# K and V stores moved from SyncE's queue to GpSimd's, loads issued at the first free slot, weight gradients stored whole

## The chip, the cores and the metric

The kernel runs on one core of one Trainium2 chip. The core has five instruction queues that matter here: TensorE (PE), VectorE (DVE), ScalarE (ACT), GpSimd (POOL) and SyncE (SP). Transfers between memory (HBM) and on-chip memory (SBUF) are issued from a queue and carried by 16 DMA engines that serve the whole core. The metric is the device time of one launch in microseconds (us). Before the change it is 729.72 us, the median of three runs (728.75 to 731.86).

## The reference

The reference is the forward pass and the gradient of a decode block with one token (x has 640 numbers). A layer norm of x feeds two branches that are added to x: attention of one query per head over a cache (32 heads, 8192 keys, 128 numbers each), and a gated MLP (640 to 1728 and back). In short:

```
q = xn @ wq                       # 32 heads x 128
p_h = softmax(q_h . K_h / sqrt(128));  o_h = p_h @ V_h
out = x + concat(o) @ wo + (silu(xn@w1) * (xn@w3)) @ w2
# gradients of everything, from grad_out:
dV_h = outer(p_h, do_h)           # 8192 x 128 per head
dK_h = outer(u_h, q_h)            # u_h = p_h * (V_h.do_h - p_h.(V_h.do_h))
dwq, dwo, dw1, dw3, dw2 and dx    # dw* are outer products too
```

All tensors are bf16. K and V are 2 MB (2,097,152 bytes) per head each, and the gradients dK and dV are just as large. So 64 tiles of 2 MB are read and 64 are written; the profile counts 151.34 MB read and 151.34 MB written in all.

## The kernel before

**Slots.** SBUF holds ten slots of 2 MB (`free_slots`, L116). A slot is a tile of 128 partitions by 8192 numbers (16,384 bytes per partition). K or V of a head is loaded into a slot, used there, and then overwritten in place by its own gradient (`outer`, L464: two DVE instructions of 128x4096 per tile, L466), which is stored from the same slot (`store`, L477). The slot then goes to the end of `free_slots` and takes a later head's K or V (`load_next`, L122). Four of the slots first hold the MLP's weights (mA to mD); the MLP is done between heads 1 and 2 (`mlp`, L557), its weight gradients are stored from GpSimd, and the slots then join the others.

**A head.** `head(h)` (L746) writes the order of the work by hand. PE transposes pieces of K (`T`, L314, PE L318 with the ACT copy L320), multiplies them with the query (`Mp`, L339), then the same for V; DVE does the softmax; PE sums with the tile as the moving operand (`wsum`, L433). The outer products of head h-1 run during head h: `outers_a` (L734) at its start makes dV, stores it, and makes half of dK; `outers_b` (L740) in its middle makes the rest of dK and stores it. The first transposes of the next head's K lie at the end of a head. So K of a head is held from shortly before its head to the middle of the next, and V from the middle of its head to the start of the next.

**Weight groups.** wq and wo are loaded by groups of four heads (`load_group`, L109: 640 KB each, three buffers per tensor in `wpool`). Group g+1 is first read in the third head of group g (`prep_do`, DVE L257, called from `side_v`) and multiplied in its fourth (`prep_q`). When a group is done, wo is overwritten by its gradient (`fin_wo`, L518) in the first head of the next group, and wq in pieces (`fin_wq`, L524) in the second and third. The last of the five pieces is made in the middle of the third head; then wq's gradient is stored and group g+3 is loaded into the freed buffers, from GpSimd.

**Queues.** A transfer is issued when its queue reaches it and everything it waits for has come. Within a queue nothing overtakes. Before the change SP issues all loads and all stores of K and V (`fifo`, L104), in the order store, load, store, load; a load waits there until the store that empties its slot has landed. `load_next` issues a load only when at least three slots are free (`lag[0] = 3`, L160), so a load goes into the slot whose store was issued two stores earlier. GpSimd's queue issues the loads and stores of the weight groups and of the MLP's gradients. The weight gradients are split (`store_group`, L505): for groups 1 to 5, wq's 128 rows go as 5 rows and 121 rows from GpSimd and 2 rows from SP; in the last group both tensors go as 68 rows from SP and 5 and 55 rows from GpSimd.

Transfers from SP are described by hardware (the profile's queue q1, hardware_dynamic), those from GpSimd by software on GpSimd (q0, software_dynamic). Each of the 16 DMA engines keeps one list of packets for each of the two. Completion is counted on eight marks in turn for each of the two kinds, so a transfer also waits for the landing of the eighth one before it of its kind.

Of the kernel before, what the change touches and what calls it, by code (L numbers as in the profile page):

```python
# [16 lines left out]
P = 128  # L17
# [4 lines left out]
def kernel(  # L22
# [22 lines left out]
    nc = tc.nc  # L45
# [8 lines left out]
    GH = 4  # L54
    NG = H // GH
    GW = GH * DH
# [19 lines left out]
    dkc = out_2.rearrange("b h (p j) d -> (b h) p (j d)", p=P)  # L76
    dvc = out_3.rearrange("b h (p j) d -> (b h) p (j d)", p=P)
    wq_v = A_wq.rearrange("(ci p) n -> p ci n", p=P)
    wo_v = A_wo.rearrange("(h p) c -> p h c", p=P)
    dwq_v = out_4.rearrange("(ci p) n -> p ci n", p=P)  # L80
    dwo_v = out_5.rearrange("(h p) c -> p h c", p=P)
# [22 lines left out]
    def fifo(out_, in_):  # L104
        nc.sync.dma_start(out_, in_)
# [3 lines left out]
    def load_group(g, eng):  # L109
        wq_g = wpool.tile([P, NC, GW], BF16, name="wq_g", tag="wq_g")  # L110
        eng.dma_start(wq_g[:], wq_v[:, :, g * GW:(g + 1) * GW])
        wo_g = wpool.tile([P, GH, D], BF16, name="wo_g", tag="wo_g")
        eng.dma_start(wo_g[:], wo_v[:, g * GH:(g + 1) * GH, :])
        grp[g] = dict(wq=wq_g, wo=wo_g)

    free_slots = [kvpool.tile([P, KVN], BF16, name=f"kv{i}", tag=f"kv{i}") for i in range(NSLOT)]  # L116
    kv_tiles = {}
    pending = [("K", h) if k == 0 else ("V", h) for h in range(H) for k in range(2)]

    lag = [1]  # L120

    def load_next():  # L122
        if not pending or len(free_slots) < lag[0]:
            return
        kind, h = pending.pop(0)
        t = free_slots.pop(0)
        fifo(t[:], (kc if kind == "K" else vc)[h])
        kv_tiles[(kind, h)] = t

    load_next()  # L130
    load_group(0, nc.sync)
    for _ in range(3):
        load_next()
# [22 lines left out]
    fifo(w3b, w3_v[:, NA, :])  # L156
    for _ in range(2):
        load_next()

    lag[0] = 3  # L160

    ident_f = consts.tile([P, P], F32, name="ident_f")
    make_identity(nc, ident_f[:])
# [83 lines left out]
    def prep_new(g):  # L247
        G_ = grp[g]
        G_["cb"] = wpool.tile([P, 2, GH], BF16, name="cb", tag="cb")
        G_["do"] = wpool.tile([P, GH], F32, name="do_c", tag="do_c")  # L250
        G_["cm"] = wpool.tile([P, 2, 2, GH, 2], BF16, name="cm_g", tag="cm_g")
        G_["od"] = wpool.tile([P, GH, 2], F32, name="od_g", tag="od_g")

    def prep_do(g, hh):
        G_ = grp[g]
        junk = small.tile([P, D], BF16, name="side", bufs=1)
        nc.vector.scalar_tensor_tensor(junk[:], G_["wo"][:, hh, :], 1.0, g_bc[:], ALU.mult, ALU.mult,  # L257
                                       accum_out=G_["do"][:, hh:hh + 1])
        if hh == GH - 1:
            nc.vector.tensor_copy(G_["cb"][:, 1, :], G_["do"][:])  # L260
# [24 lines left out]
    def prep_cm(g, ps):  # L285
        nc.vector.tensor_tensor(grp[g]["cm"][:].rearrange("p t a h m -> p (t a h) m"),
                                ps.unsqueeze(2).to_broadcast([P, 4 * GH, 2]),
                                mask2.unsqueeze(1).to_broadcast([P, 4 * GH, 2]), ALU.mult)
# [188 lines left out]
    def store(kind, h):  # L477
        t = kv_tiles.pop((kind, h))
        if kind == "K":
            hd.pop(h)  # L480
        fifo((dkc if kind == "K" else dvc)[h], t[:])
        free_slots.append(t)
        load_next()

# [17 lines left out]
        for hh in range(GH):  # L502
            out_row(G_["od_bf"][:, hh, 0:1], G_["wo"][:, hh, :])

    def store_group(g, dst, t, split=False):  # L505
        if split:
            for lo, hi in ((0, 5), (5, 126)):
                nc.gpsimd.dma_start(dst[lo:hi], t[lo:hi])
            fifo(dst[126:P], t[126:P])
            return  # L510
        if g < NG - 1:
            nc.gpsimd.dma_start(dst, t[:])
            return
        fifo(dst[0:68], t[0:68])
        for lo, hi in ((68, 73), (73, P)):
            nc.gpsimd.dma_start(dst[lo:hi], t[lo:hi])

    def fin_wo(g):  # L518
        G_ = grp[g]
        for hh in range(GH):  # L520
            nc.vector.tensor_scalar(G_["wo"][:, hh, :], g_bc[:], G_["od"][:, hh, 0:1], None, ALU.mult)
        store_group(g, dwo_v[:, g * GH:(g + 1) * GH, :], G_["wo"])

    def fin_wq(g, ci):  # L524
        G_ = grp[g]
        wq_g, dqb = G_["wq"], G_["dqb"]
        nc.vector.scalar_tensor_tensor(wq_g[:, ci, :], wq_g[:, ci, :], 1.0, dqb, ALU.mult, ALU.mult,  # L527
                                       accum_out=dxa[:, ci, g:g + 1])
        nc.vector.tensor_scalar(wq_g[:, ci, :], dqb, xn_col[:, ci:ci + 1], None, ALU.mult)
        if ci == NC - 1:  # L530
            store_group(g, dwq_v[:, :, g * GW:(g + 1) * GW], wq_g, 1 <= g <= 5)
            grp.pop(g)
            if g + 3 < NG:
                load_group(g + 3, nc.gpsimd)

    def wrow(wi, ci):
        if ci < NA:
# [146 lines left out]
    def side_k(h):  # L684
        g, hh = divmod(h, GH)
        if hh == 1 and g > 0:
            fin_wq(g - 1, 0)
        elif hh == 2 and g > 0:
            fin_wq(g - 1, 3)
        elif hh == 3 and g + 1 < NG:  # L690
            prep_do(g + 1, 1)

    def side_m(h):
        g, hh = divmod(h, GH)
        if hh == 0 and g > 0:
            fin_od(g - 1)
        elif hh == 1 and g > 0:
            fin_wq(g - 1, 1)
        elif hh == 2 and g > 0:
            fin_wq(g - 1, 4)  # L700
        elif hh == 3 and g + 1 < NG:
            prep_do(g + 1, 2)
            prep_do(g + 1, 3)

    def side_v(h):
        g, hh = divmod(h, GH)
        if hh == 0 and g > 0:
            fin_wo(g - 1)
        elif hh == 1 and g > 0:
            fin_wq(g - 1, 2)  # L710
        elif hh == 2 and g + 1 < NG:
            prep_new(g + 1)
            prep_do(g + 1, 0)
        elif hh == 3 and g + 1 < NG:
            prep_cm(g + 1, hd[h]["m"][:, 324:324 + 4 * GH])

    def side_pe1(h):
        g, hh = divmod(h, GH)
        if hh == 0 and g > 0:
            fin_pe(g - 1)  # L720
        elif hh == 3 and g + 1 < NG:
            prep_q(g + 1)
# [11 lines left out]
    def outers_a(h):  # L734
        outer_v(h, 0, J // 2)
        outer_v(h, J // 2, J)
        store("V", h)
        outer_k(h, 0, J // 2)

    def outers_b(h):  # L740
        outer_k(h, J // 2, J)
        store("K", h)
# [3 lines left out]
    def head(h):  # L746
# [39 lines left out]
        Mp(h, "V", 4)  # L786
        side_pe2(h)
        side_v(h)
        if nxt:
            fill_qz(h + 1)  # L790
# [45 lines left out]
    fin_od(NG - 1)  # L836
    fin_pe(NG - 1)
    fin_wo(NG - 1)
    for ci in range(NC):
        fin_wq(NG - 1, ci)  # L840
# [58 lines left out]
```

## Time and profile before

| | before |
|---|---|
| median of three runs | 729.72 us |
| the profiled execution's own time | 730.06 us |
| its span in the profile | 728.3 us |
| PE, DVE, ACT, POOL busy | 82%, 63%, 52%, 5% |
| bytes moved, mean rate | 303.53 MB, 417 GB/s |
| mean granted TensorE clock | 0.927 |

The page cuts the span into 40 slices; a digit is the busy share of an engine in tenths, and the DMA line is the mean of the 16 DMA engines. Queue lines give packets, megabytes and the time that the packets took as a share of 16 engines' span. A line of waits gives the waiting engine and line, what it waited for, the total in us, the number of waits and the longest. A line of a table of windows gives, for a stretch of the span, the busy time of PE, PE's weight loads, DVE, ACT and POOL with their instruction counts, then the granted clock, the DMA share and GB/s. Lines of DMA issues end with the median time from issue to landing.

### The profile page before, as it was taken

What the parts mean: (1) busy time and instruction counts of PE and PEld (TensorE: products, weight loads), DVE (VectorE), ACT (ScalarE), POOL (GpSimd) and SP (SyncE); (2) the same over time, 40 slices, a digit from 0 to 9 for tenths busy, and PEclk for the clock granted to TensorE, in tenths of its full rate; (3) what the DMA queues carried; (4) which work ended last, traced back from release to release, by engine and by line L of the source; (5) the groups of instructions that cost most, each with busy time, mean ns of one, the idle gap of its engine ahead of it and who ended that gap; (6) DMA issues with size and microseconds to landing.
All of it is one profiled execution on the core that took longest, in us unless ns stands there. A gap on an engine that the chain in (4) does not pass through costs nothing.

```text
span 728.3 us, 12951 instructions
## 1 busy us (share of the span) xinstructions
PE 600.8 (82%) x5193; PEld 375.6 (52%) x5193; DVE 460.1 (63%) x811; ACT 375.7 (52%) x727; POOL 35.0 (5%) x52
## 2 busy tenths in 40 slices
PE   3989589999999999877986889878896987988840
PEld 2547456665566556544554555445563555644520
DVE  4169646677767886767556746556755665677482
ACT  3640736665666656544554546455562555645410
POOL 0010110000100000000010000000000000000000
PEclk9996799999999999999999989999998999999975
DMA  9999999999999999999999999999999999999996
GB/s 347 398 409 424 427 428 428 413 427 425 418 409 429 427 426 424 423 429 422 425 425 427 431 420 427 421 427 432 410 428 424 428 425 422 429 424 430 429 415 239
DMA packets 28358, 303.53 MB, mean 417 GB/s; under 512 B 3481, under 2 KB 5532, under 8 KB 11658
## 3 DMA queue, kind: packets, MB, share of 16 engines
q1 hardware_dynamic: 22022, 277.14, 90.4%
q0 software_dynamic: 6272, 25.56, 8.8%
q8 instruction: 41, 0.67, 0.4%
q14 instruction: 19, 0.16, 0.1%
q10 hardware_dynamic: 4, 0.00, 0.0%
HBM read 151.34 MB, written 151.34 MB: 416 GB/s over the span
## 4 chain that ended last, share of the span: by engine, by line
DMA 57%; PE 33%; DVE 5%; ACT 2%; issue 1%; SPq 0%; ACTq 0%; DVEq 0%
DMA out_dram<-kv 30%; DMA kv<-in_A_k_cache_dram 18%; PE pT L318 15%; DMA kv<-in_A_v_cache_dram 7%; PE sA L339 4%; PE X L433 3%; PE dA L339 3%; DVE kv L466 2%; PE m L356 2%; DMA wo_g<-in_A_wo_dram 2%; ACT KT L320 1%; PE gu_ps L562 1%; PE dh_ps L573 1%; DVE side L257 0%; PE pT L266 0%
## 5 line engine op out<-in xcount | busy, mean ns | idle before, releaser
L320 ACT COPY KT<-pT 128x512 f32<-128x512 f32 x512 | 287.7, 587 | 230.9 <-PE pT L318 210.3
L318 PE MATMUL pT<-ident_f,kv 128*128 128x128 f32 x2048 | 306.6, 289 | 61.6 <-DMA kv<-in_A_k_cache_dram 29.9
L318 PEld LDWEIGHTS pT<-ident_f,kv 128*128 128x128 f32 x2048 | 236.2, 148 | 155.1 <-issue 59.6
L466 DVE TENSOR_TENSOR kv<-qd,U 128x4096 bf16<-128x4096 bf16 x64 | 146.0, 2283 | 0.0
L466 DVE TENSOR_TENSOR kv<-qd,P 128x4096 bf16<-128x4096 bf16 x64 | 143.5, 2283 | 0.0
L433 PE MATMUL X<-kv,Z 128*32 128x512 bf16 x1024 | 93.5, 402 | 1.8 <-DVE Z L450 1.8
L339 PE MATMUL sA<-KT,qz 128*32 128x512 bf16 x512 | 83.9, 408 | 0.0
L339 PE MATMUL dA<-KT,qz 128*32 128x512 bf16 x512 | 83.3, 404 | 0.0
L416 DVE SCALAR_TENSOR_TENSOR U<-m,P 128x64 bf16<-128x64 f32 x32 | 7.5, 234 | 83.0 <-PE m L356 83.0
L382 DVE TENSOR_REDUCE mrow<-m 128x1 f32<-128x64 f32 x32 | 7.2, 223 | 75.1 <-PE m L356 75.0
L339 PEld LDWEIGHTS <-qz 128*32 128x32 bf16 x1024 | 29.6, 95 | 40.4 <-issue 37.7
L433 PEld LDWEIGHTS <-Z 128*32 128x32 bf16 x1024 | 32.4, 99 | 33.8 <-issue 5.7
L356 PE MATMUL m<-selc,KT 64*128 64x64 f32 x256 | 30.7, 243 | 8.6 <-ACT KT L346 8.6
L356 PEld LDWEIGHTS m<-selc,KT 64*128 64x128 f32 x256 | 21.7, 145 | 30.4 <-ACT KT L346 21.6
L376 ACT CAST qd<-pT 128x256 bf16<-128x256 f32 x32 | 11.9, 372 | 40.3 <-DVE kv L466 28.8
L389 DVE TENSOR_REDUCE negM<-m 128x1 f32<-128x128 f32 x32 | 9.3, 291 | 33.2 <-PE m L386 33.2
L527 DVE SCALAR_TENSOR_TENSOR wq_g<-wq_g,side 128x512 bf16<-128x512 bf16 x40 | 27.3, 682 | 0.0
L257 DVE SCALAR_TENSOR_TENSOR side<-wo_g,g_bc 128x640 bf16<-128x640 bf16 x32 | 26.2, 819 | 1.4 <-DMA wo_g<-in_A_wo_dram 1.1
L448 DVE SCALAR_TENSOR_TENSOR U<-m,P 128x128 bf16<-128x128 f32 x32 | 11.4, 355 | 15.8 <-PE m L446 15.8
L406 DVE RECIPROCAL rZ<-m 128x1 f32<-128x1 f32 x32 | 5.3, 166 | 24.2 <-PE m L400 24.2
L346 ACT COPY KT<-dA 64x512 f32<-64x512 f32 x32 | 18.6, 583 | 2.6 <-PE dA L339 2.6
L346 ACT COPY KT<-sA 64x512 f32<-64x512 f32 x32 | 18.6, 580 | 2.3 <-PE sA L339 2.1
(164 smaller groups left out, 377.4 us busy)
## 6 DMA issues: line engine op xcount, KB each, us to landing
out_dram<-kv SPq DMA_DIRECT2D x64, 2048.0 KB, 30.9
kv<-in_A_k_cache_dram SPq DMA_DIRECT2D x32, 2048.0 KB, 27.9
kv<-in_A_v_cache_dram SPq DMA_DIRECT2D x32, 2048.0 KB, 26.0
wq_g<-in_A_wq_dram POOLq DMA_DIRECT2D x7, 640.0 KB, 13.5
wo_g<-in_A_wo_dram POOLq DMA_DIRECT2D x7, 640.0 KB, 19.6
out_dram<-wo_g POOLq DMA_DIRECT2D x7, 640.0 KB, 15.6
kv<-in_B_w_dram SPq DMA_DIRECT2D x2, 1728.0 KB
out_dram<-kv POOLq DMA_DIRECT2D x2, 1728.0 KB, 23.2
```

Of the source, the lines that this page charges most:

```text
L257: nc.vector.scalar_tensor_tensor(junk[:], G_["wo"][:, hh, :], 1.0, g_bc[:], ALU.mult, ALU.mult, accum_out=G_["do"][:, hh:hh + 1])
L318: nc.tensor.transpose(pT[:, k * P:(k + 1) * P], W3[:, 4 * c + k, :], ident_f[:])
L320: nc.scalar.copy(KT[:].rearrange("p k w -> p (k w)"), pT[:])
L339: nc.tensor.matmul(S_[kind][q:q + QW, :], lhsT=S_["qz"][:, o:o + QW], rhs=KTb[c][:, par, :], start=(c0 == 0 and par == 0), stop=(c0 == NCH ...
L346: nc.scalar.copy(XS[0:QH].rearrange("p k w -> p (k w)"), S_.pop(kind)[0:QH, :])
L356: nc.tensor.matmul(S_["m"][:, b0:b0 + 4 * J].rearrange("p (x c k t) -> p k x c t", x=4, k=4, t=2)[:, k], lhsT=XS[0:QH, k, :], rhs=selc[0:Q ...
L376: nc.scalar.copy(qd[:].rearrange("p a d -> p (a d)"), hd[h].pop("ps_r"))
L389: nc.vector.tensor_reduce(S_["negM"][:], S_["m"][:, 2 * J:2 * J + P], AX.X, ALU.max, negate=True)
L433: nc.tensor.matmul(xg["X"][q:q + QW, :], lhsT=Z[:, o:o + QW], rhs=W[:, N4 * i:N4 * (i + 1)], start=(slot == 0 and i < 4), stop=(slot == NS ...
L448: nc.vector.scalar_tensor_tensor(S_["U2"][:], S_["V"][:, 0:J].unsqueeze(2).to_broadcast([P, J, 2]), S_["m"][:, OC + NS:OC + NS + 1], S_["P ...
L466: nc.vector.tensor_tensor(dst[:, lo * DH:hi * DH].rearrange("p (j a b) -> p j a b", a=DH // 2, b=2), vec.rearrange("p (a b) -> p a b", b=2 ...
L527: nc.vector.scalar_tensor_tensor(wq_g[:, ci, :], wq_g[:, ci, :], 1.0, dqb, ALU.mult, ALU.mult, accum_out=dxa[:, ci, g:g + 1])
```

## The change

Four things change; the arithmetic and the order of the work on PE, DVE and ACT stay as they are.

1. Stores of dK and dV are issued from GpSimd. SP issues only loads (and the two small output rows at the end).
2. `lag` goes: `load_next` issues a load as soon as one slot is in `free_slots`. That is right after the store of that slot, so each load on SP waits for the store that was issued just before it on GpSimd.
3. The weight gradients are stored whole, 128 rows in one transfer, all from GpSimd.
4. A weight group is loaded one head later: in the fourth head of a group (`side_v`) instead of in the middle of the third, just after wq's store.

GpSimd's queue thereby has, for each group of four heads, eight stores of 2 MB, one store of wo's and one of wq's gradient and the two loads of a weight group, in program order.

```
@@ load_next
-    lag = [1]
-        if not pending or len(free_slots) < lag[0]:
+        if not pending or not free_slots:
             return
...
-    lag[0] = 3
@@ store(kind, h)
-        fifo((dkc if kind == "K" else dvc)[h], t[:])
+        nc.gpsimd.dma_start((dkc if kind == "K" else dvc)[h], t[:])
         free_slots.append(t)
         load_next()
@@
-    def store_group(g, dst, t, split=False):
-        if split:
-            for lo, hi in ((0, 5), (5, 126)):
-                nc.gpsimd.dma_start(dst[lo:hi], t[lo:hi])
-            fifo(dst[126:P], t[126:P])
-            return
-        if g < NG - 1:
-            nc.gpsimd.dma_start(dst, t[:])
-            return
-        fifo(dst[0:68], t[0:68])
-        for lo, hi in ((68, 73), (73, P)):
-            nc.gpsimd.dma_start(dst[lo:hi], t[lo:hi])
@@ fin_wo
-        store_group(g, dwo_v[:, g * GH:(g + 1) * GH, :], G_["wo"])
+        nc.gpsimd.dma_start(dwo_v[:, g * GH:(g + 1) * GH, :], G_["wo"][:])
@@ fin_wq
         if ci == NC - 1:
-            store_group(g, dwq_v[:, :, g * GW:(g + 1) * GW], wq_g, 1 <= g <= 5)
+            nc.gpsimd.dma_start(dwq_v[:, :, g * GW:(g + 1) * GW], wq_g[:])
             grp.pop(g)
-            if g + 3 < NG:
-                load_group(g + 3, nc.gpsimd)
@@ side_v
+        if hh == 3 and g > 0 and g + 2 < NG:
+            load_group(g + 2, nc.gpsimd)
```

## The prediction

> **What bounds the kernel now.** I read the slices first, then the queue lines, then windows, and only then the waits.
>
> ```profile
> DMA  9999999999999999999999999999999999999996
> GB/s 347 398 409 424 427 428 428 413 427 425 418 409 429 427 426 424 423 429 422 425 425 427 431 420 427 421 427 432 410 428 424 428 425 422 429 424 430 429 415 239
> q1 hardware_dynamic: 22022, 277.14, 90.4%
> q0 software_dynamic: 6272, 25.56, 8.8%
> ```
>
> The 16 DMA engines are busy in every slice but the last. That is the bound: 303.53 MB at the 428 GB/s of a good slice is 709 us, and the span is 728.3. Of the 19 us between, the first three slices lose 18.2 x (81 + 30 + 19) / 428 = 5.5 us, the last two 18.2 x (13 + 189) / 428 = 8.6, and the rest about 5.
>
> ```profile
> 140.00:660.00 520.00, 453.80 (x3902) 280.02 (x3899) 340.01 (x565) 287.84 (x575) 22.74 (x28) 0.96 1.01 424
> 712.00:720.00 8.00, 0.93 (x3) 0.58 (x3) 3.45 (x17) 0.00 (x0) 1.34 (x2) 0.50 0.93 343
> 720.00:728.30 8.30, 0.00 (x0) 0.00 (x0) 0.00 (x0) 0.00 (x0) 0.00 (x0) 0.50 0.28 98
> ```
>
> In these windows the DMA share stands before GB/s at the end: 1.01 for 520 us, while PE has 66 us free. After 720 us no engine computes and the DMA engines fall silent one after another. The trace keeps the completion marks of all 16 for each transfer: for the last store of dK they come 0, 0.1, 0.2, 0.2, 0.5, 2.1, 3.8, 6.6 and then up to 14.5 us after the first, and the last mark is 1.0 us before the span ends. So the most loaded DMA engine sets the end; it never runs dry.
>
> ```profile
> SPq L105 <- DMA out_dram<-kv: 453.0, 50, 14.9
> PE pT L318 <- DMA kv<-in_A_k_cache_dram: 29.9, 16, 3.9
> PE pT L318 <- DMA kv<-in_A_v_cache_dram: 29.1, 15, 4.3
> out_dram<-kv SPq DMA_DIRECT2D x64, 2048.0 KB, 30.9
> kv<-in_A_k_cache_dram SPq DMA_DIRECT2D x32, 2048.0 KB, 27.9
> ```
>
> SP stands 453 us on landings of stores, which looks like the fat that the change cuts. It is not: the DMA engines are full meanwhile. A head moves 8.39 MB of K and V and 0.65 MB of weights, 21.3 us at 424 GB/s. Ten slots at one per 10.65 us give each a cycle of 106.5 us: 31 store, 27 load, about 28 held by compute (K some 38, V some 19), and the 20 left are two slots idling because of `lag` (2 x 10.65). Taking that idleness away deepens a queue that is never empty.
>
> **The change, part by part.** The sum is against the profiled execution, 730.06 us (span 728.3 and 1.8 around it; 0.3 over the median).
>
> *Stores on GpSimd, cost per byte.* 64 stores, 134.2 MB, pass from q1 to q0. The nearest row is the MLP's w2 gradient, stored from GpSimd with rows of 15,360 bytes beside K and V loads:
>
> ```profile
> DMA packets 228, 3.42 MB, mean 428 GB/s; under 512 B 12, under 2 KB 12, under 8 KB 12
> q0 software_dynamic: 115, 1.77, 51.6%
> q1 hardware_dynamic: 113, 1.65, 48.3%
> ...
> DMA packets 357, 5.16 MB, mean 430 GB/s; under 512 B 42, under 2 KB 42, under 8 KB 42
> q1 hardware_dynamic: 357, 5.16, 101.5%
> ```
>
> The first window, 80 to 88 us, has just the mix that the change makes everywhere, half software stores and half hardware loads: 428 GB/s. The second, 128 to 140 us, is hardware alone: 430. By the packets, 15,360 bytes take 573.7 ns on q0 and 16,384 take 611 on q1, the same 26.8 GB/s per engine. Cost 0. The far bound is q0's price over the whole page: 8.8% for 25.56 MB against 90.4% for 277.14, 5.5% dearer per MB. q1's 134.2 MB took 43.8% of the span, 319 us; 5.5% of it is +17.6. I take 0, for q0's page price is made by packets of 4 and 5 KB, and keep 17.6 for the range; below, -2 for 430 against 428 either way.
>
> *Issue.* SP loses 64 issues of 0.33 to 0.44 us, GpSimd gains 64 at 0.56 (the w2 store) to 0.88 (a whole wq store): up to 56 us, POOL from 35 to some 90 us of 728. Nothing computes behind GpSimd; cover is the store queue, several transfers deep. Of its other work, the second gate copy (L832, done at 52.2) stands before the stores of head 1, the first of which SP issued at 57: 0.
>
> A rule speaks against this part. The Trainium skill, SBUF — State Buffer, Who interferes with whom: GpSimd shares a port pair with VectorE, and certain VectorE modes lock it out of writing descriptors; a page example goes from about 620 to 3100 ns. As an estimate from that page, 64 stores late by 2.5 us make 160 us of GpSimd time, and still 0 in the sum while stores queue for 40 us. The issues above beside a busy VectorE show no such stretch.
>
> *First free slot, loads alone.* With two lists on each DMA engine, served in turn as the window's 51.6 and 48.3% show, a load behind few others gets half the rate: 2 x 4.9 us for 2 MB plus some 2, about 12 instead of 27. The slot's cycle stays 106.5, so what load and lag give up the store gets: 106.5 - 28 - 12 = 66 at most, I expect 40 to 60. No bytes go: 0. What the PE waits of 59 us lose comes back elsewhere, for bytes pace the heads. Early, PE paces heads at 18 us (in the chain of waits the same group starts at 119.1, 136.9 and 155.1), and 8.39 MB in 18 us is 466 GB/s, more than the engines move, so they stay full there too.
>
> *The weight group one head later.* Each group's wq store now queues behind stores of 2 MB on the same list, and the load on GpSimd waits for its landing; behind it on GpSimd stand the next dV and dK stores, and behind those SP's loads. Store: five queued x 9.8 = 49. Load: the three stores issued in between, 29, and its own packets, 10 x (0.16 + 0.61) + 8 x (0.20 + 0.61) = 14. Together 92 us, and from one third head to the next there are 4 x 21.3 = 85. So `prep_do` (L257), which waited 1.1 us in all, may wait some 7 us in each of five groups, 36 us of DVE and PE. Cover: the stores queued meanwhile, three at least, 14.7 us of DMA work. 0 as long as one wait is shorter than that; 36 if the cover is gone; no gain.
>
> *Weight gradients whole.* Here the end moves. Of the five split stores of wq, the packets tell who carries what: 55 packets of 3072 bytes, the odd end of 11 rows of five 1 KB pieces, so in each split 11 DMA engines carry 11 rows and five carry one of the five others. Whole, all carry 8. The five are those whose marks come first, the 11 include the last. The 11 lose 3 rows = 15,360 bytes per split, at 159 ns per 4096 bytes 0.60 us, x 5 = -3.0. In the last group they had 5 rows of each tensor and get 8: 2 x 0.60 = +1.2. Together -1.8. The five gain 7 rows x 0.2 x 5 = 7.0, and the one of them that the 68 rows miss 2.8 more; 0.5 + 9.8 = 10.3 after the first mark, still before 14.5 - 1.8 = 12.7. So bounds are -3.0 and 0.
>
> *End.* Last comes wq's store on GpSimd instead of dK's on SP: 0 to +1, taken 0, since both wait on the same laden engine.
>
> Sum: 730.06 - 1.8 = 728.3; against the median, 728.0.
>
> **Rivals.**
> 1. *The software list is dearer* (slower). Every store pays q0's page price: 729.7 + 17.6 = 747, at half of it 738. It decides when the 1024 packets of 16 KB that each DMA engine carries (64 x 8 of stores and as many of loads) take over 616 ns (1024 x 5.4 ns = 3.7 + 1.8), or the stores alone over 622. For it: 134 MB were never on q0. The Trainium skill, DMA: Bandwidth & Descriptors, Latency and other measured facts, has DMA engines 7 and 15 usually slower with transfers issued from GpSimd, without a figure, and no view here tells the engines apart. Against: the 428 GB/s window.
> 2. *Late weights* (slower). The wait at L257 outlasts the queued stores: up to 729.7 + 36 = 766. It decides when one wait passes 14.7 us.
> 3. *The DMA engines come out even* (faster). The marks' mean is 6.0 after the first, the last 14.5; if separate lists level them, 8.5 go: 721. Against: levelling needs other work per engine, and rows are equal anyway.
> 4. *PE's 59 us of waits are won* (faster). 671 us is under 303.53 MB at 432, the best slice: 703. Excluded.
> 5. *Nothing but names moves*: each load still waits for a store, and the split matters as little as 0.2%: 729.7.
>
> **How the numbers follow.** The reckoning above has 0.50, with a range of its own of 724 to 733 (half of the runs' spread, 1.6, and some 3 for unevenness drawn anew); rival 1 0.17, rival 2 0.10, rival 3 0.15, rival 5 0.08. 0.5%, 3.6 us, is about what can be told from no change, so faster is under 726.1 and slower over 733.4. The first case gives 0.11 faster, 0.35 same, 0.04 slower; rivals 1 and 2 slower, 3 faster, 5 same. Together 0.26, 0.43, 0.31. 721 takes in rival 3; 741 takes in rival 1 at half price and leaves 0.14 above.
>
> **What would show it.** Right: q0 near 160 MB at 425 GB/s or more from 140 to 660 us; loads near 12 us, dK and dV stores 40 to 60; PE waits less for K and V, DVE L257 appears behind wo's load, POOL L111 waits longer for wq's store. Wrong: slices under 9 in the DMA line, a q0 share above its bytes, or marks of the last store spread by more than 15 us.

## The result and the profile after

The changed kernel takes 736.07 us (median of 5 runs, 735.85 to 736.23), the kernel before 729.72 us in the same comparison (5 runs, 727.23 to 731.86). The ratio is 1.0089, with a 95% interval of 1.0065 to 1.0114: 0.9% slower. The profiled execution spans 734.1 us against 728.3, so 5.8 us of span are to be found.

The queue table of the changed kernel (queue and kind: packets, MB, share of the time of 16 DMA engines) says that they are not in the price of a byte:

```profile
q0 software_dynamic: 14944, 160.52, 52.0%
q1 hardware_dynamic: 12126, 142.17, 46.0%
```

52.0 / 160.52 is 0.324% per MB on GpSimd's software list, 46.0 / 142.17 is 0.324% on the hardware list. The software list now holds 134 MB more, at the same price.

The windows of the changed kernel (stretch, its length, then busy time of PE, PEld, DVE, ACT and POOL, TensorE clock, share of the DMA engines, GB/s) show a steady rate and a long tail (here and below, `...` stands for lines left out):

```profile
140.00:660.00 520.00, 454.72 (x3898) 279.29 (x3900) 340.68 (x565) 287.61 (x576) 46.45 (x74) 0.95 1.01 426
...
712.00:720.00 8.00, 0.93 (x3) 0.58 (x3) 2.27 (x12) 0.00 (x0) 0.87 (x1) 0.50 0.77 313
...
720.00:722.00 2.00, 0.00 (x0) 0.00 (x0) 0.00 (x0) 0.00 (x0) 0.00 (x0) 0.50 0.20 81
...
724.00:726.00 2.00, 0.00 (x0) 0.00 (x0) 0.00 (x0) 0.00 (x0) 0.00 (x0) 0.50 0.06 25
...
728.00:730.00 2.00, 0.00 (x0) 0.00 (x0) 0.00 (x0) 0.00 (x0) 0.00 (x0) 0.50 0.07 27
```

From 140 to 660 us the DMA engines move 426 GB/s (424 before). From 724 to 730 us the share is 0.06 to 0.07: one DMA engine of 16 is at work and fifteen are done. The completion marks say the same. Those of the last dK store come 0, 0.3, 0.4, 0.5, 0.6 and so on up to 7.0 and 9.2 us after the first, and the last one at 15.7, so the last DMA engine is 6.5 us behind the second last; before, this distance was 3.0 us. In the same stretch of 720 to 722 us, before still had 0.67 of its DMA engines busy, and its stretch with one engine left is short:

```profile
720.00:722.00 2.00, 0.00 (x0) 0.00 (x0) 0.00 (x0) 0.00 (x0) 0.00 (x0) 0.50 0.67 232
722.00:724.00 2.00, 0.00 (x0) 0.00 (x0) 0.00 (x0) 0.00 (x0) 0.00 (x0) 0.50 0.39 134
724.00:726.00 2.00, 0.00 (x0) 0.00 (x0) 0.00 (x0) 0.00 (x0) 0.00 (x0) 0.50 0.08 33
```

A second part of the loss lies behind all transfers. The last mark of any transfer comes at 731.0 us in the changed kernel, 3.1 us before its span ends, and at 727.4 us before, 0.9 us before the end. In the changed kernel the last store is GpSimd's, and GpSimd's closing DRAIN instruction, which all engines wait for at the end, is done only at 733.2 us, 2.2 us after that mark. Before, SyncE's store was last, and GpSimd's DRAIN was done at 726.4 us, ahead of it.

The waits of the changed kernel (engine and line, what it waited for: us in all, times, longest) hold what was moved about; the DMA engines are full meanwhile:

```profile
SPq L105 <- DMA out_dram<-kv: 605.0, 58, 22.2
...
POOL wq_g L111 <- DMA out_dram<-wq_g: 126.5, 5, 33.8
...
DVE side L253 <- DMA wo_g<-in_A_wo_dram: 16.2, 5, 4.8
...
PE pT L314 <- DMA kv<-in_A_k_cache_dram: 34.5, 15, 5.1
...
PE pT L314 <- DMA kv<-in_A_v_cache_dram: 15.2, 9, 4.8
```

Its DMA issues (KB each, median us from issue to landing) answer to those shown of before:

```profile
out_dram<-kv POOLq DMA_DIRECT2D x64, 2048.0 KB, 45.2
kv<-in_A_k_cache_dram SPq DMA_DIRECT2D x32, 2048.0 KB, 18.7
kv<-in_A_v_cache_dram SPq DMA_DIRECT2D x32, 2048.0 KB, 22.3
```

Loads land sooner (27.9 us before for K), stores later (30.9 before), as the slot's cycle demands, and TensorE waits 49.7 us for K and V instead of 59.0. DMA engines that are full pay nothing for that.

To tell dearer transfers from a ragged end, the tables below split a span in two. "Moving" is the sum of the durations of all DMA packet records of a profile, divided by 16; "idle" is the span less that, the time in which an average DMA engine had nothing to do, most of it at the end: first while it waited for the last DMA engine, and then between the last mark and the end of the span. (A packet's record starts 3 or 4 ns before the former one ends, so idle is some 6 us more in truth, in every kernel nearly alike.)

| profile | span | moving | idle | of it after the last mark |
|---|---|---|---|---|
| before | 728.3 | 725.6 | 2.7 | 0.9 |
| changed | 734.1 | 722.7 | 11.4 | 3.1 |

The change saves 2.9 us of moving and loses 8.7 in idle time: 2.2 after the last mark and 6.5 of evenness before it. The sum is the 5.8 us.

### The profile page after: what moved, and what is told of

Read it like the earlier page. It is cut to its first block, busy times and chain, and to the rows that moved or that the text cites. A ratio compares the mean times of both kernels' runs of the same rounds, so it can differ in the third digit from the quotient of the medians.

```text
span 734.1 us, 13013 instructions
## 1 busy us (share of the span) xinstructions
PE 601.6 (82%) x5186; PEld 374.7 (51%) x5193; DVE 460.3 (63%) x811; ACT 375.5 (51%) x727; POOL 64.7 (9%) x109
## 3 DMA queue, kind: packets, MB, share of 16 engines
q0 software_dynamic: 14944, 160.52, 52.0%
q1 hardware_dynamic: 12126, 142.17, 46.0%
## 4 chain that ended last, share of the span: by engine, by line
DMA 30%; PE 28%; issue 17%; another core or an unknown queue 11%; DVE 7%; ACT 3%; POOL 1%; SPq 0%; POOLq 0%; ACTq 0%; DVEq 0%
DMA wo_g<-in_A_wo_dram 16%; PE pT L314 13%; DMA out_dram<-kv 8%; DMA kv<-in_A_k_cache_dram 4%; PE sA L335 4%; PE X L429 2%; PE dA L335 2%; DMA kv<-in_A_v_cache_dram 2%; DVE kv L462 2%; PE m L352 1%; ACT kv L624 1%; DVE side L253 1%; PE gu_ps L543 1%; PE dh_ps L554 1%
## 5 line engine op out<-in xcount | busy, mean ns | idle before, releaser
L429 PE MATMUL X<-kv,Z 128*32 128x512 bf16 x1024 | 97.4, 414 | 1.4 <-DVE Z L446 1.4
L335 PE MATMUL sA<-KT,qz 128*32 128x512 bf16 x512 | 82.4, 401 | 0.0
L477 POOL DMA_DIRECT2D out_dram<-kv x64 | 34.7, 543 | 393.6 <-DVE kv L462 184.7
L253 DVE SCALAR_TENSOR_TENSOR side<-wo_g,g_bc 128x640 bf16<-128x640 bf16 x32 | 26.2, 820 | 16.6 <-DMA wo_g<-in_A_wo_dram 16.2
L444 DVE SCALAR_TENSOR_TENSOR U<-m,P 128x128 bf16<-128x128 f32 x32 | 11.4, 356 | 15.4 <-PE m L442 15.4
## 6 DMA issues: line engine op xcount, KB each, us to landing
out_dram<-kv POOLq DMA_DIRECT2D x64, 2048.0 KB, 45.2
kv<-in_A_k_cache_dram SPq DMA_DIRECT2D x32, 2048.0 KB, 18.7
kv<-in_A_v_cache_dram SPq DMA_DIRECT2D x32, 2048.0 KB, 22.3
```

The costliest lines, as they stand in the source:

```text
L335: nc.tensor.matmul(S_[kind][q:q + QW, :], lhsT=S_["qz"][:, o:o + QW], rhs=KTb[c][:, par, :], start=(c0 == 0 and par == 0), stop=(c0 == NCH ...
L429: nc.tensor.matmul(xg["X"][q:q + QW, :], lhsT=Z[:, o:o + QW], rhs=W[:, N4 * i:N4 * (i + 1)], start=(slot == 0 and i < 4), stop=(slot == NS ...
L444: nc.vector.scalar_tensor_tensor(S_["U2"][:], S_["V"][:, 0:J].unsqueeze(2).to_broadcast([P, J, 2]), S_["m"][:, OC + NS:OC + NS + 1], S_["P ...
L477: nc.gpsimd.dma_start((dkc if kind == "K" else dvc)[h], t[:])
```

## The experiments

Four theories are told apart. Theory 1: issuing the K and V stores from GpSimd lets one DMA engine fall behind. Theory 2: the split weight gradients of before took rows from just the DMA engine that would be last, and storing them whole gives them back. Theory 3: the late weight groups, or the loads without `lag`, cost it. Theory 4 is theory 1 made definite: the stores in the software list widen the spread of the 16, beside whatever theory 2 takes. Each kernel is timed beside its own runs of the kernel before, whose medians lie between 728.15 and 729.14 us (729.72 for the changed kernel), so ratios are the safest comparison. Span, moving and idle are those of one profile each; e4_lag and the changed kernel, equal in time, differ by 1 us in idle.

| kernel | median us | ratio to before, 95% interval | span | moving | idle | after the last mark |
|---|---|---|---|---|---|---|
| e2_whole: weight gradients whole | 732.00 | 1.0043 (1.0026 to 1.0059) | 730.3 | 722.5 | 7.8 | 1.2 |
| e13_late: and weight groups late | 732.08 | 1.0048 (1.0031 to 1.0065) | 730.3 | 722.1 | 8.2 | 1.2 |
| e14_first: and stores of heads 0 to 15 on GpSimd | 734.78 | 1.0088 (1.0070 to 1.0105) | 732.3 | 723.3 | 9.0 | 1.2 |
| e15_last: instead those of heads 16 to 31 | 733.96 | 1.0077 (1.0056 to 1.0097) | 732.0 | 722.1 | 9.9 | 2.3 |
| e4_lag: all of them | 736.44 | 1.0095 (1.0073 to 1.0116) | 735.8 | 723.4 | 12.4 | 3.1 |
| changed: and `lag` gone | 736.07 | 1.0089 (1.0065 to 1.0114) | 734.1 | 722.7 | 11.4 | 3.1 |
| e6_stores: e4_lag with early weight groups | 742.78 | 1.0200 (1.0180 to 1.0220) | 741.2 | 728.3 | 12.9 | 3.1 |
| e9_swap: before, pieces of the splits swapped | 736.68 | 1.0119 (1.0098 to 1.0139) | 735.3 | 724.9 | 10.3 | 1.1 |
| e1_split: changed, with the splits of before | 741.72 | 1.0176 (1.0142 to 1.0209) | 739.8 | 730.7 | 9.1 | 1.2 |
| e16_split_swap: e1_split, pieces swapped | 750.33 | 1.0291 (1.0258 to 1.0324) | 749.3 | 735.0 | 14.3 | 3.2 |

### The weight gradients alone, and the splits put back

e2_whole, an edit of the kernel before (the same for the wo gradient):

```diff
-            store_group(g, dwq_v[:, :, g * GW:(g + 1) * GW], wq_g, 1 <= g <= 5)
+            nc.gpsimd.dma_start(dwq_v[:, :, g * GW:(g + 1) * GW], wq_g[:])
```

> The kernel before with the weight gradients stored whole from GpSimd and nothing else changed. The prediction's own step and theory 1: 727 to 729 us (the step says 1.8 us less than 729.7). Theory 2: 734 to 736 us, with one DMA engine alone at the end for some 6 us.

Measured: 732.00 us, ratio 1.0043. It is slower, where the prediction's step and theory 1 had it 1.8 us faster or equal, and short of the 734 to 736 us of theory 2. Moving falls by 3.1 us and idle grows by 5.1. The windows of e2_whole (columns as above) show one DMA engine finishing alone in this kernel too, with every K and V store on SyncE:

```profile
720.00:722.00 2.00, 0.00 (x0) 0.00 (x0) 0.00 (x0) 0.00 (x0) 0.00 (x0) 0.50 0.34 139
...
724.00:726.00 2.00, 0.00 (x0) 0.00 (x0) 0.00 (x0) 0.00 (x0) 0.00 (x0) 0.50 0.07 29
726.00:728.00 2.00, 0.00 (x0) 0.00 (x0) 0.00 (x0) 0.00 (x0) 0.00 (x0) 0.50 0.06 25
```

e1_split is the other way round, the changed kernel with `store_group` of before:

```diff
-            nc.gpsimd.dma_start(dwq_v[:, :, g * GW:(g + 1) * GW], wq_g[:])
+            store_group(g, dwq_v[:, :, g * GW:(g + 1) * GW], wq_g, 1 <= g <= 5)
```

> The changed kernel with the weight gradients split over the two lists as before; everything else stays changed. Theory 1 (one DMA engine falls behind because the K and V stores are issued from GpSimd, whatever the splits do): the straggler stays, and its gap to the second last at the last stores, 6.5 us in the changed kernel, moves by 3 us at most: 733 to 739 us. Theory 2 (the splits had relieved just that DMA engine: 7 rows less in each of five splits, 7.0 us, and 2.8 us in the last group): the gap closes and the time falls to 727 to 730 us.

Measured: 741.72 us, above both expectations. Idle falls to 9.1 from 11.4, but 1.9 of these 2.3 us lie after the last mark, and moving grows by 8.0 us: packets are stretched. From 130 to 700 us, 256 packets of 16,384 bytes take over 760 ns, against 116 in the changed kernel. From 480 to 490 us, fifteen loads of 16,384 bytes take 798 to 1275 ns instead of 611; what is under way from GpSimd then is the load of a weight group (issued at 479.0 and 479.9 us), so these aren't stretched by the pieces themselves. So putting the splits back doesn't mend the changed kernel.

### Does it matter which DMA engines a split relieves?

e9_swap leaves everything of before as it is, down to the packets, and only swaps the two GpSimd pieces of each split:

```diff
-            for lo, hi in ((0, 5), (5, 126)):
+            for lo, hi in ((0, 121), (121, 126)):
...
-        for lo, hi in ((68, 73), (73, P)):
+        for lo, hi in ((68, 123), (123, P)):
```

> The kernel before with the two GpSimd parts of each split in the other order: 121 rows and then 5, in place of 5 and then 121. If the splits help because they take rows from just the DMA engine that is last (theory 2), and the parts are dealt out to the DMA engines in turn, then other five are relieved and the last one may now carry 3 rows more per split: 733 to 736 us. If it does not matter which five are relieved: 729 us as before.

Measured: 736.68 us, ratio 1.0119; theory 2 said 733 to 736. Moving is the same as before (724.9 against 725.6), idle goes from 2.7 to 10.3. The windows of e9_swap:

```profile
140.00:660.00 520.00, 451.44 (x3848) 278.58 (x3852) 338.20 (x559) 286.23 (x571) 22.77 (x28) 0.95 1.01 425
...
720.00:722.00 2.00, 0.00 (x0) 0.00 (x0) 0.00 (x0) 0.00 (x0) 0.00 (x0) 0.50 0.51 165
...
728.00:730.00 2.00, 0.00 (x0) 0.00 (x0) 0.00 (x0) 0.00 (x0) 0.00 (x0) 0.50 0.10 32
...
732.00:734.00 2.00, 0.00 (x0) 0.00 (x0) 0.00 (x0) 0.00 (x0) 0.00 (x0) 0.50 0.06 20
```

The rate is that of before, 425 GB/s, and the last DMA engine works alone at 0.06. In each split eleven DMA engines carry 11 rows and five carry one, as the prediction read from the packets; whole stores give 8 to each. By the prediction's own price of 0.2 us a row, a DMA engine that 5 rows first relieve carries 7 rows less in each of five splits than with whole stores, 7.0 us, and one that is not relieved carries 3 rows more, 3.0 us. Idle went from 2.7 (5 rows first) to 7.8 (whole, e2_whole) and 10.3 (121 rows first): 5.1 and then 2.5 us. That fits theory 2, where the DMA engine that is last with whole stores is among the five that 5 rows first relieve: relieved it leaves the end to another one, and in the other order it carries more. So the splits of before were worth their place because 5 rows went first; in the other order they cost more than no split at all (e2_whole).

Which five these are, by their place in the order of the marks, isn't shown. Each DMA engine finishes a K or V transfer every 4.9 us (8 packets of 611 ns), while the marks of one transfer lie 7 to 19 us apart around the splits of before. So marks that come within 5 us of each other belong to different transfers, and their order doesn't tell which DMA engine is behind.

### The K and V stores on GpSimd

e4_lag keeps `lag`; e13_late is e4_lag with the K and V stores on SyncE again, so that the two differ in one thing:

```diff
-        nc.gpsimd.dma_start((dkc if kind == "K" else dvc)[h], t[:])
+        fifo((dkc if kind == "K" else dvc)[h], t[:])
```

> The changed kernel with the rule kept that a load waits for three free slots. Theories 1 and 2: the straggler is as before, 734 to 738 us, no difference. Against both: if loads that run ahead are what lets one DMA engine fall behind, its gap at the end shrinks from 6.5 us and the time falls to some 730 us.

> e2_whole (732.0 us) with the weight groups loaded one head later. It differs from e4_lag (736.4 us) only in who issues the K and V stores, SyncE here and GpSimd there. Theory 4 (those stores in the software list widen the spread): 731 to 733 us. If the late weight groups, and not the list, made the 4 us from e2_whole to the changed kernel: 735 to 737 us.

Measured: e4_lag 736.44 us, the same as the changed kernel, so taking `lag` away costs and brings nothing here. e13_late 732.08 us, the same as e2_whole, so the late weight groups cost nothing as long as SyncE stores K and V. That leaves the 4 us between e13_late and e4_lag to who issues the stores. Moving hardly differs (722.1 and 723.4); idle is 8.2 and 12.4. Theory 3 falls. Of theory 4, it stands that the stores on GpSimd cost some 4 us; that they widen the spread is half of it at most. Of the 4.2 us of idle between the two profiles, 1.9 come after the last mark, where GpSimd's DRAIN is waited for (done 2.2 us after the last mark in e4_lag, 1.9 before it in e13_late), and 2.3 before; for the changed kernel against e13_late it is 1.9 and 1.3. And the spread of the last dK store's marks is wide without these stores as well: 17.2 us in e2_whole and 17.1 in e13_late, against 14.3 in e4_lag and 15.7 in the changed kernel.

Are these 4 us gathered all along, or are they those of the last stores in flight? e14_first and e15_last put half of the heads on GpSimd:

```diff
-        fifo((dkc if kind == "K" else dvc)[h], t[:])
+        (nc.gpsimd if h < 16 else nc.sync).dma_start((dkc if kind == "K" else dvc)[h], t[:])
```

> e13_late (732.1 us) with the K and V stores of heads 0 to 15 issued by GpSimd, those of heads 16 to 31 by SyncE; e4_lag has all of them on GpSimd (736.4 us). If one DMA engine falls behind all along with software stores, and keeps its lag: half of the 4.3 us, about 734 us. If only the stores in flight at the end count: 732 us.

> The other half: heads 0 to 15 on SyncE, 16 to 31 on GpSimd. Lag gathered all along: about 734 us. Only the end counts: 736 us, as with all of them on GpSimd.

Measured: 734.78 and 733.96 us. Either half costs about half of it in microseconds, also the first one, whose last K or V store from GpSimd is issued at 384 us, nearly 350 us before the end. "Only the end counts" asked for 732 and 736. The first is out, for the interval of e14_first lies just above that of e13_late; the second isn't, for those of e15_last and e4_lag overlap. How the first half comes to cost 2.7 us isn't settled. Between the profiles it is 2.0 us, 1.2 of it in moving and 0.8 in idle. A lag that is kept can explain only a part: the distance of the last DMA engine from the second last is 3.5 to 5.8 us for stores issued between 425 and 460 us in e14_first, against 2.1 to 3.0 in e13_late, but after 640 us it is 7.1 to 9.4 against 6.1 to 8.0. So one DMA engine falls behind all through the run with all K and V stores on SyncE too, and what the stores on GpSimd added shrinks to about 1 us. In e15_last, 1.1 us more than in e13_late come after the last mark.

e16_split_swap asks whether it is the same DMA engine that is last with GpSimd's stores. It is e1_split with its pieces swapped as in e9_swap.

> e1_split (the changed kernel with the splits of before, 741.7 us) with 121 rows first and 5 after. If the DMA engine that is last with software stores is one of the five that 5 rows first relieve, as in the kernel before: it now carries more, 745 us or more (e9_swap lost 7.6 us of span by this). If it is one of the other eleven: no worse than e1_split, 738 to 742 us.

Measured: 750.33 us. The order of the pieces is worth 9.5 us of span here: 5.2 in idle (14.3 against 9.1, of which 2.1 after the last mark), 4.3 in moving. So this order is the worse one in this kernel as well, which is what theory 2 expects if it is the same DMA engine that is last; moving, on which the theory has nothing, makes up nearly half of it.

### The late weight groups, with the stores on GpSimd

e6_stores takes from the changed kernel only the whole weight gradients and the stores on GpSimd; against e4_lag:

```diff
-        if hh == 3 and g > 0 and g + 2 < NG:
-            load_group(g + 2, nc.gpsimd)
...
             grp.pop(g)
+            if g + 3 < NG:
+                load_group(g + 3, nc.gpsimd)
```

> The kernel before with two parts of the change: weight gradients whole, and the K and V stores issued by GpSimd; the three-slot rule and the early weight groups are as before. It differs from e2_whole (732.0 us) in who issues the K and V stores, and from e4_lag (736.4 us) in when the weight groups are loaded. Theory 4 (the stores in the software list widen the spread of the 16 DMA engines at the end): 735 to 737 us, one DMA engine alone for 6 us or more at the end. Theory 3 (late weight groups cost it): 731 to 733 us.

Measured: 742.78 us, outside both ranges and worse than the changed kernel by 6.7. The waits of GpSimd in e6_stores, and then the line of its slices with GB/s:

```profile
POOL wq_g L111 <- DMA out_dram<-wq_g: 219.9, 5, 52.0
```

```profile
GB/s 350 400 413 418 426 429 411 420 429 432 425 332 428 427 431 417 332 430 428 431 369 412 430 428 428 341 431 426 431 428 346 431 430 429 428 428 430 428 427 270
```

GpSimd stands up to 52.0 us at the weight load until wq's store has landed, with the K and V stores queued behind it in program order; the slots run out, the loads stop, and one slice in every four or five falls to 332 to 369 GB/s. With the load one head later (e4_lag) the same wait is 34.4 us at most and the slices have no such hole. So that part of the change is what makes the stores on GpSimd bearable; it isn't a cost.

### What the stores on SyncE, ScalarE or both do

e3_sp is the changed kernel with the K and V stores on SyncE, without `lag`.

> The changed kernel with the K and V stores issued by SyncE again; weight gradients whole, loads at the first free slot and weight groups late stay as changed. Theory 1: no straggler, 727 to 731 us. Theory 2: 734 to 737 us, for the whole weight gradients are still there. A third theory (late weight groups, 16 us of waits for them in the changed kernel, and no lag) says 734 to 737 us too, and is told from theory 2 by where the DMA engines have holes.

Measured: 939.91 us, ratio 1.2907, which no theory had. The waits of SyncE's queue in e3_sp:

```profile
SPq L105 <- DMA out_dram<-kv: 776.5, 54, 26.9
```

Without `lag`, a load goes into the slot whose store has just been issued. SyncE serves in order, so it stands until that store has landed, and the next store can't be issued meanwhile; the slices from 141 to 890 us lie between 276 and 349 GB/s. On SyncE alone, `lag` is needed; it is the stores' move to GpSimd that makes it needless. It says nothing on theories 1 and 2.

e7_half puts the V stores on GpSimd and the K stores on SyncE, on the base of e6_stores; e8_act has ScalarE issue all of them.

> e6_stores with only the V stores on GpSimd and the K stores on SyncE again. Theory 4, if the effect grows with the bytes in the software list: half way between e2_whole and e6_stores, 733 to 735 us. If what counts is that loads and stores stand in separate lists at all: 732 us or less, since here they are mixed on SyncE again.

> e6_stores with the K and V stores issued by ScalarE, so in a hardware list of their own, apart from the loads. ScalarE stands at each store until VectorE has written the tile, which the DMA engines, the bound, may not feel. Theory 4: spread at the end as in e2_whole, 731 to 734 us. If two separate lists widen the spread whoever fills them: 735 to 738 us with one DMA engine alone at the end. If ScalarE's waits break the heads' pace: over 740 us with holes in the DMA line from 140 to 660 us, and nothing is told.

Measured: 744.26 us (ratio 1.0219) and 836.11 us (1.1461). Both break the flow of work: e7_half has GpSimd at the weight load for up to 26.2 us and slices down to 387 GB/s before the last two, e8_act runs at 379 GB/s from 140 to 660 us. They tell nothing of lists. Whether a hardware list apart from the loads would have spared the 4 us stays open, as does whether it would have spared the 1.9 after the last mark.

### Moving rows by one large store

e10_relief splits one V store of the changed kernel (head 28) into 5 and 121 rows on GpSimd and 2 on SyncE, e11_burden swaps the two, and e12_whole_relief does the same as e10_relief in e2_whole.

```diff
+        if kind == "V" and h == 28:
+            for lo, hi in ((0, 5), (5, 126)):
+                nc.gpsimd.dma_start(dvc[h][lo:hi], t[lo:hi])
+            fifo(dvc[h][126:P], t[126:P])
+        else:
             nc.gpsimd.dma_start((dkc if kind == "K" else dvc)[h], t[:])
```

> The changed kernel with one of the 64 K and V stores, the V store of head 28, in three pieces: 5 rows and then 121 rows from GpSimd, 2 rows from SyncE. If 5 and 121 rows go to 5 and to 11 DMA engines, five carry 7 rows of 16 KB less (7 x 0.61 = 4.3 us), among them the one that is last (theory 2, by e9_swap), and the others 3 rows more (1.8 us). The last one ends 4.3 us earlier and the second last, 6.5 us ahead of it in the changed kernel, 1.8 later: 731.8 us, 731 to 733. If the slow DMA engine is not among the five, or one store doesn't reach the end: 736 to 738 us.

> e10_relief with the two GpSimd pieces in the other order, 121 rows and then 5. Theory 2: the DMA engine that is last carries 3 rows more, 736.1 + 1.8 = 738 us, 737 to 739.5. If the order doesn't matter: as e10_relief.

> e2_whole (732.0 us: the kernel before with the weight gradients whole) with the V store of head 28 in the pieces of e10_relief; all other K and V stores stay on SyncE. There the last DMA engine stands 6.3 us behind the second last. Theory 2: 4.3 us less, 727.7 us, 726.5 to 729. If not: 731 to 734 us.

Measured: 743.43, 741.53 and 732.85 us (ratios 1.0203, 1.0176, 1.0054; moving 726.4, 726.2 and 724.2). All three are slower than what they start from (736.1 and 732.0), and none does what theory 2 asked of it. In e10_relief, where the last DMA engine was to end earlier, the last mark of the last dK store is 10.5 us behind the second last (6.5 in the changed kernel). The premise of these runs does not show in the records: strung together, the packets of most DMA engines show 8 rows of the split store, not 11, and in e11_burden one DMA engine alone runs ahead after it (the marks of the next stores start 0 and 7.1 us). So rows of 16,384 bytes weren't dealt 5 and 11 here, and these runs neither support nor refute theory 2. And a single split store costs 1.7 to 3.7 us of moving. A version faster than both kernels did not come of it.

## Why the prediction was wrong

It said 728.0 us and no measurable change, with 721 to 741 as the range; it is 736.07, inside the range, but on the slower side, which had 0.31. Step by step:

- *Stores on GpSimd, cost per byte: 0.* Right as far as bytes go: 0.324% per MB in either list. Packets of 16,384 bytes take 616.7 ns in the software list and 615.3 in the hardware one from 130 to 690 us (618.2 before), at the 616 from which rival 1 was to decide. (That threshold was reckoned from 611, the time of an undisturbed packet; the mean was above it before the change as well, so it decides nothing.) But this part was costed by bytes alone, and the move costs about 4 us all the same (e4_lag against e13_late): about half after the last mark, the rest in evenness and moving. The prediction's own sign for being wrong, marks of the last store more than 15 us apart, came: 15.7 for the last dK store. It points at the whole weight gradients rather than here, for e13_late, with these stores on SyncE, has 17.1.
- *Weight gradients whole: -1.8.* This is the step that failed first. "The five are those whose marks come first, the 11 include the last" was inferred from the order of marks after the splits, and from it followed that the DMA engine that is last loses 3 rows per split and that the five, given 7 back, stay ahead of it. Measured alone, the step is worth +0.43% (1.0026 to 1.0059), some 3 us, made of -3.1 moving and +5.1 idle in the profiles: evenness got worse, and in e2_whole the last DMA engine works alone from 724 us on. As e9_swap argues, a DMA engine that ends last without the relief is among the five; their start of 0.5 us after the first mark was then too early for it. Which one it is stays open.
- *Issue: 0.* Right: 64 stores at 0.53 us, POOL from 35.0 to 64.7 us rather than to 90. The Trainium skill (SBUF — State Buffer, Who interferes with whom) has certain modes of VectorE lock GpSimd out of writing descriptors. No such stretch shows here: the longest of these 64 issues is 0.71 us, beside a VectorE that is 63% busy.
- *First free slot: 0.* Right: e4_lag and the changed kernel are alike. Stores land in 45.2 us, within the 40 to 60 expected. Loads take 18.7 and 22.3 us and not 12.
- *The weight group one head later: 0.* Its waits came smaller than the 7 us each that were reckoned (16.2 us in five, 4.8 at most, hidden), and e13_late shows no cost. "No gain" was wrong: without it, the kernel with the stores on GpSimd is 6.3 us slower (e6_stores against e4_lag).
- *End: 0.* This term was too small, with bounds of 0 to +1. From the last mark of any transfer to the end of the span it is 3.1 us in the changed kernel and 0.9 before, so +2.2: with GpSimd's store last, GpSimd's DRAIN is waited for, 2.2 us after the mark in the changed kernel, e4_lag and e6_stores alike. Why it takes so long there isn't known; in e1_split, where GpSimd's store is last too, it is done after 0.4 us. The rest of the sum rested on one thought, that the DMA engine that sets the end keeps its place. Rival 3 let the unevenness shrink. No case let it grow, except as some 3 us of "unevenness drawn anew".

In all, by the ratios: +0.4% from the whole weight gradients, nothing from the late groups, +0.5% from the stores on GpSimd (the longer end included), nothing from `lag`: 0.9%.

Why one DMA engine stays behind, and whether more so with software stores, is not settled. The Trainium skill (DMA: Bandwidth & Descriptors, Latency and other measured facts) has DMA engines 7 and 15 usually slower with transfers issued from GpSimd. The runs agree that one is behind the others at the end, but it is so with all K and V stores on SyncE as well (e2_whole, e13_late), and the records do not number the DMA engines. What such stores add before the last mark, 1.3 to 2.3 us of idle, is not far above the 1.0 us by which two profiles of equally fast kernels differ.

## What to carry to other kernels

When the DMA engines are the bound, read two things apart: what the packets cost, and how long an average DMA engine stands idle while the last one finishes; a change can leave the first alone and lose everything in the second. Then look behind the last completion mark too: here over a third of the lost span lies there. An odd-looking split of a transfer may be there for the dealing of rows: find out from the records which DMA engines carry what before you call it overhead, and don't infer it from the order of their marks. Who issues a store, when the next transfer in the same program order waits, and what rule keeps loads behind belong together; whole weight gradients and stores on GpSimd without the late weight load cost 2% together, and the changed kernel without those stores on GpSimd, loads at the first free slot kept, 29%.

## What the hardware did that was not expected

- The order of two pieces of a store, 5 rows and 121 or 121 and 5, with the same bytes and the same packets, is worth 1.2% of the kernel (e9_swap). Moving is the same; all of it is idle time while the last DMA engines finish.
- One DMA engine falls behind the others all through a run, also with all K and V stores on SyncE: in e13_late the last mark of a store lies 2.1 to 3.0 us behind the second last for stores issued from 425 to 460 us, and 6.1 to 8.0 after 640 us.
- With GpSimd's store last, 3.1 us pass between the last completion mark and the end of the span, against 0.9 to 1.2 with SyncE's (changed, e4_lag and e6_stores against before, e2_whole and e13_late). In e1_split it is 1.2 with GpSimd's store last too.
- With split stores, packets take longer: moving grows by 8.0 us for the splits in e1_split, by 3.7 for a single V store in e10_relief.
- In the two kernels whose 16 go in step, packets are slower, not faster: in e3_sp the marks of late stores lie within 2.5 us and moving is 814.7 us for the same bytes, in e8_act within 0.2 us and 770.5. That the one makes the other was not tried.
